# The last 64 tokens of a sequence on all 128 rows of TensorE, in an attention and two MLPs on one Trainium2 core

## The chip, the cores and the metric

The kernel runs on one core of a Trainium2 chip. TensorE multiplies a stationary operand, which a weight load (PEld in the profile) puts into its array of 128 rows and 128 columns, by a moving operand that streams past it (PE in the profile). The contraction runs over the rows. A product over 64 values uses 64 of the rows and is shown as 64*128 in the profile, where the first number is the rows and the second the columns that the stationary operand fills. VectorE (DVE), ScalarE (ACT) and GpSimd (POOL) do the rest of the arithmetic, and SyncE (SP) issues the DMAs, in the order of its queue.

The metric is the device time of one execution in microseconds (us), the median of several runs.

## The reference

An attention in two steps over 8 batches of 8 heads with 576 tokens of 64 values each, in float32, and two MLPs behind it:

```python
def sm_attn(qq, kk, vv):
    s = scale * np.matmul(qq, kk.transpose(0, 1, 3, 2))
    s = s - np.max(s, axis=-1, keepdims=True)
    a = np.exp(s)
    a = a / (np.sum(a, axis=-1, keepdims=True) + 1e-09)
    return np.matmul(a, vv)
p_packed = sm_attn(p, k, v)             # p: 32 rows a head
out = sm_attn(q, p_packed, p_packed)    # 576 rows a head
...
xn = x / rms * rms_g                    # x: 4608 tokens of 512 values
g = xn @ w_gate
x = silu(g) * (xn @ w_val) @ w_out      # 1536 hidden
h = x @ w_in
out = (h * sigmoid(1.702 * h)) @ w_out  # 2048 hidden
```

576 tokens are four chunks of 128 and one of 64. The 64 tokens of that last chunk are what the change is about.

## The kernel before, in words

**The order of the whole.** The attention is cut into 16 chains, one for each batch and each group g of four heads (`chains`, line 146). Chains 0 to 3 (`n < LEAD`) run at the start, spread out by `start` (line 485), which gives each step a time by hand and sorts by it. Chains 4 to 15 run beside the first MLP: `stages` (line 526) lists their steps in order, and the loop at lines 1285 to 1322 hands out one step whenever the first MLP has issued a set amount of TensorE work. So TensorE's queue holds the attention's transposes and products in the middle of the first MLP's products (`prods` line 679, `gateval` line 712, `project` line 748). The second MLP (lines 1068 and 1140) follows without any attention in it. A Tile scheduler with a model of the timeline turns this program into the queues of the engines; some instructions are held in program order, among them all loads of chains 4 and up (line 185).

**One chain.** `load_kp`, `load_v` and `load_q` bring the four heads' k, p, v and q. Each has the last 64 tokens in a load of its own: `kn[:REST, NC - 1]` (lines 197 and 206), `vs[1]` (line 226), `qn[:REST, NC - 1]` (line 240), with NC = 5 and REST = 64. In chains 0 to 3 k comes first as one wide tile, kw, and VectorE puts it in order (line 200). SP issues all loads.

`heads_t` (line 285) transposes k or q, for a pair of heads a and one half e of the chunks: half 0 holds chunks 0 and 1, half 1 holds chunks 2, 3 and 4. Each transpose (line 297) loads the chunk as the stationary operand and streams the identity past it. For chunk 4 the stationary operand is 64 rows high and the identity is cut to 64x64. `scores` (line 308) gives the scores of the packed rows, `s1` their softmax weights e1. `a_t` (line 333) transposes e1 in the same two halves; for chunk 4 the stationary operand has 128 rows and 64 columns, and the 64 rows that come out are copied by two instructions of their own (line 345), apart from those for the other chunks (line 343). `split_v` (line 243) splits v into a high and a low part from chain 4 on, in two pieces: the four full chunks, and chunk 4 on 64 partitions (lines 251 to 255). `pv` (line 347) sums weights by v over the five chunks; from chain 4 on each chunk takes three products (high by high, high by low, low by high), and those of chunk 4 are 64 rows high (line 355). In chains 0 to 3 the operands are plain float32, and the profile shows two instructions for a chunk.

`x` (line 431) makes the rows' sums of squares; its last chunk has 128 rows and 64 columns. `scale` (line 463) transposes the inverse norms ri for each chunk; for the last one (line 474) the stationary operand again has 64 rows.

**Which instructions have 64 rows.** Two transposes of k and two of q in each chain (a = 0 and 1 with e = 1), the products of chunk 4 in `pv`, and one transpose in `scale` for each of the 8 batches.

Of the kernel before, what the change touches and what calls it, by code (L numbers as in the profile page):

```python
# [26 lines left out]
def fl(t):  # L27

    return t.bitcast(F32)
# [3 lines left out]
def tile_pack_attention__then__two_mlps(  # L33
# [14 lines left out]
    nc = tc.nc  # L48
    B, H, S, D = q.shape
# [8 lines left out]
    P = 128  # L58
    HS = S // 2
    TS = 2 * S // 3  # L60
    NC = -(-S // P)
    REST = S - (NC - 1) * P
# [85 lines left out]
    def attention(at, first, lp, psum, getL, getAT):  # L148
# [31 lines left out]
        def load(n, dst, src):  # L180


            i = nc.sync.dma_start(dst, src)
            if n >= LEAD:
                tc.keep_in_program_order(i)

        def load_kp(n):
            at = early(n)
            b, g = chains[n]
            h0, odd = HG * g, b % 2  # L190
            nb = KQ if n < LEAD else 2
            kn = at.tile([P, NC, HG, D], F32, tag="kq", name="kn", bufs=nb)
            rest = k[b, h0 : h0 + HG, S - REST :].rearrange("h p d -> p h d")
            if n < WIDE:
                kw = at.tile([P, HG, NC - 1, D], F32, tag="kq", name="kw", bufs=nb)
                load(n, kw, k[b, h0 : h0 + HG, : S - REST].rearrange("h (p c) d -> p h c d", c=NC - 1))
                load(n, kn[:REST, NC - 1], rest)
                for a in range(2):
                    hs = slice(2 * a, 2 * a + 2)
                    nc.vector.tensor_copy(kn[:, : NC - 1, hs].rearrange("p c h d -> p h c d"), kw[:, hs])  # L200
            else:
                for h in range(HG):
                    load(n, 
                        kn[:, : NC - 1, h, :], k[b, h0 + h, : S - REST].rearrange("(p c) d -> p c d", c=NC - 1)
                    )
                load(n, kn[:REST, NC - 1], rest)
            pb = at.tile([P, HG, D], F32, tag="pb", name="pb", bufs=bufs(n))
            for s in range(2):
                hs = h0 + 2 * (s ^ odd)
                load(n,   # L210
                    pb[64 * s : 64 * s + 64],
                    p[b, hs : hs + 2].rearrange("h n d -> (h n) d").unsqueeze(1).to_broadcast([64, HG, D]),
                )
            st[n].update(kn=kn, pb=pb)

        def load_v(n):
            at = early(n)
            b, g = chains[n]
            tag, nb = ("kq", KQ) if n < LEAD else ("vn", 1)
            vn = at.tile([P, NC, HG, D], F32, tag=tag, name="vn", bufs=nb)  # L220
            vn = vn.rearrange("p c h d -> p (c h d)")
            head = (NC - 1) * HG * D
            vs = vn[:, :head].rearrange("p (h c d) -> p h c d", h=HG, d=D), vn[:REST, head:]
            hs = slice(HG * g, HG * g + HG)
            load(n, vs[0], v[b, hs, : S - REST].rearrange("h (p c) d -> p h c d", c=NC - 1))
            load(n, 
                vs[1].rearrange("p (h d) -> p h d", h=HG), v[b, hs, S - REST :].rearrange("h p d -> p h d")
            )
            st[n]["vn"] = vn

        def load_q(n):
            b, g = chains[n]
            qn = at.tile([P, NC, HG, D], F32, tag="kq", name="qn", bufs=2)
            hs = slice(HG * g, HG * g + HG)
            rest = q[b, hs, S - REST :].rearrange("h p d -> p h d")
            for h in range(HG):
                load(n, 
                    qn[:, : NC - 1, h, :], q[b, HG * g + h, : S - REST].rearrange("(c p) d -> p c d", p=P)
                )
            load(n, qn[:REST, NC - 1], rest)  # L240
            st[n]["qn"] = qn

        def split_v(n):
            at = early(n)
            vn = st[n]["vn"]
            if full(n):
                st[n]["v"] = (vn,)
                return
            vh, vl = (at.tile([P, NC * HG * D], F32R, tag=f"v{x}", name=f"v{x}") for x in "hl")
            head = (NC - 1) * HG * D  # L250
            for part in ((slice(None), slice(head)), (slice(REST), slice(head, NC * HG * D))):
                i = nc.scalar.copy(vh[part], vn[part])
                if n == LEAD:
                    tc.keep_in_program_order(i)
                nc.gpsimd.tensor_sub(vl[part], vn[part], fl(vh[part]))
            st[n]["v"] = vh, vl

        def v_of(t, c):

            head = (NC - 1) * HG * D  # L260
            if c < NC - 1:
                return t[:, :head].rearrange("p (h c d) -> p h c d", h=HG, d=D)[:, :, c, :]
            return t[:REST, head:].rearrange("p (h d) -> p h d", h=HG)

        def p_mask(n):
            at = early(n)
# [18 lines left out]
        def heads_t(n, name, a, e):  # L285

            if (a, e) == (0, 0):
                pool, nb = (early(n), bufs(n)) if name == "k" else (at, 1)
                st[n][name + "T"] = [
                    pool.tile([P, 2, S], kind(n), tag=f"T{x}", name=f"{name}T{x}", bufs=nb) for x in marks(n)  # L290
                ]
            src = st[n][name + "n"]
            ps = psum()
            cols = span(e)
            for c in GROUPS[e]:
                o = c * P - cols.start
                nc.tensor.transpose(  # L297
                    ps[:, o : o + size(c)],
                    src[: size(c), c, 2 * a : 2 * a + 2, :].rearrange("p h d -> p (h d)"),
                    ident[: size(c), : size(c)],  # L300
                )
            split([t[:, a, cols] for t in st[n][name + "T"]], ps[:, : cols.stop - cols.start], nc.vector)

# [29 lines left out]
        def a_t(n, e):  # L333
            at = early(n)
            if e == 0:
                st[n]["aT"] = [at.tile([P, NC, P], kind(n), tag=f"aT{x}", name=f"aT{x}", bufs=1) for x in marks(n)]
            e1 = st[n]["e1"]
            ps = psum()
            ps = ps.rearrange("p (c n) -> p c n", n=P)
            for i, c in enumerate(GROUPS[e]):  # L340
                nc.tensor.transpose(ps[: size(c), i], e1[:, c * P : c * P + size(c)], ident)  # L341
            c0, c1 = GROUPS[e][0], min(GROUPS[e][-1] + 1, NC - 1)
            split([t[:, c0:c1] for t in st[n]["aT"]], ps[:, : c1 - c0], nc.vector)
            if NC - 1 in GROUPS[e]:
                split([t[:REST, NC - 1] for t in st[n]["aT"]], ps[:REST, NC - 1 - c0], nc.vector)

        def pv(n):
            pool = early(n)
            b, g = chains[n]
            o = psum()[:, : HG * D]  # L350
            todo = [(c, x, y) for c in range(NC) for x, y in products(st[n]["aT"], st[n]["v"])]
            for i, (c, x, y) in enumerate(todo):
                nc.tensor.matmul(  # L353
                    o,
                    x[: size(c), c],
                    v_of(y, c),
                    start=i == 0,
                    stop=i == len(todo) - 1,
                )
            pp = kept(n, "pph") if full(n) else pool.tile([P, HG * D], F32, tag="pp", name="pp")  # L360
            nc.vector.scalar_tensor_tensor(pp, o, st[n]["r1"], mask[b % 2], op0=ALU.mult, op1=ALU.mult)
            if full(n):
                st[n].update(pp=pp, pps=(pp,))
            else:
                st[n].update(pp=pp, pps=[kept(n, f"pp{x}") for x in "hl"])
                split(st[n]["pps"], pp, nc.gpsimd)
# [96 lines left out]
        def scale(b, *es):  # L463

            ri = batch[b]["ri"]
            srcs = []
            for e in es:
                ps = psum()  # L470
                cols = span(e)
                for c in GROUPS[e]:
                    o = c * P - cols.start
                    nc.tensor.transpose(
                        ps[:, o : o + size(c)],
                        ri[: size(c), c : c + 1].to_broadcast([size(c), P]),
                        ident[: size(c), : size(c)],
                    )
                srcs.append((cols, ps[:, : cols.stop - cols.start]))
            for g in range(NG):  # L480
                for cols, src in srcs:
                    A = getAT(b // 2)[b % 2][g][:, cols]
                    nc.vector.scalar_tensor_tensor(A, A, math.sqrt(DM), src, op0=ALU.mult, op1=ALU.mult)
# [890 lines left out]
```

## Time and profile before

| | |
|---|---|
| time, median of 3 runs | 1620.88 us (1620.12 to 1622.61) |
| the profiled execution: its time | 1620.02 us |
| the profiled execution: span, first to last instruction | 1618.2 us |
| TensorE busy (PE) / its weight loads (PEld) | 1593.0 us / 1510.4 us |
| VectorE, ScalarE, GpSimd busy | 1094.5, 870.6, 915.7 us |
| granted TensorE clock, mean | 0.998 of 2.4 GHz |
| mean DMA rate | 215 GB/s |

How to read it: busy times of engines overlap, so they don't add up. A busy PE is modelled: an instruction's time reaches from its start to the modelled end of its results, and the next one starts before that. So what an instruction costs TensorE is read from the distance between starts, not from its busy time. PEld's idle time is measured between weight loads, with what ended it in brackets.

### The profile page before, as it was taken

Reading aid. Unit: us, or ns where it says so; the run is one execution under the profiler, and the core shown is the slowest. Engines: PE = TensorE matmul, PEld = TensorE weight load, DVE = VectorE, ACT = ScalarE, POOL = GpSimd, SP = SyncE. Lnnn points to the kernel's source line nnn. Section 1 sums busy time; section 2 is a strip of 40 time slices with the busy share of each in tenths; the row PEclk is TensorE's granted clock in tenths of the full one; section 3 lists DMA queues with packets and bytes.
Section 4 is the critical chain, followed back from the end, with each engine's and each line's share of the span. In section 5 each row is a group of like instructions: output and inputs, shape, how many; then the busy total and the mean of one; then the engine's idle time right before and its main releaser. Section 6 shows DMA issues by size and latency. Waiting matters only on the chain.

```text
span 1618.2 us, 29102 instructions
## 1 busy us (share of the span) xinstructions
PE 1593.0 (98%) x10608; PEld 1510.4 (93%) x10608; DVE 1094.5 (68%) x1899; ACT 870.6 (54%) x1799; POOL 915.7 (57%) x749
## 2 busy tenths in 40 slices
PE   7999999999999999999999999999999999999998
PEld 5699999999999999999999899999999999999998
DVE  5777777767777766676775567754685467468466
ACT  5677777666566655665665353534344434435432
POOL 3547777656655566563655275664466445546442
PEclk9999999999999999999999999999999999999999
DMA  9766666775556665475454887786677667888874
GB/s 263 222 175 185 210 198 215 255 222 184 180 176 210 204 193 180 150 250 204 153 204 149 316 282 241 235 248 187 183 225 248 189 186 240 288 247 252 285 232 143
DMA packets 217725, 348.21 MB, mean 215 GB/s; under 512 B 93936, under 2 KB 123632, under 8 KB 211440
## 3 DMA queue, kind: packets, MB, share of 16 engines
q1 hardware_dynamic: 217584, 346.35, 66.9%
q8 instruction: 85, 1.39, 0.4%
q14 instruction: 56, 0.46, 0.1%
HBM read 279.19 MB, written 67.11 MB: 214 GB/s over the span
## 4 chain that ended last, share of the span: by engine, by line
PE 90%; DMA 2%; DVE 2%; ACT 2%; issue 2%; POOL 1%; SPq 0%; POOLq 0%; DVEq 0%; ACTq 0%
PE ps_dn L1140 21%; PE ps_up L1068 20%; PE ps_o L748 18%; PE ps_g L712 18%; PE ps_w L679 4%; PE ps_at L308 3%; PE ps_at L297 2%; PE ps_at L353 2%; PE ps_at L443 2%; DMA kw<-in_k_dram 1%; DMA vn<-in_v_dram 1%; POOL ol L1114 1%; PE ps_at L341 0%; DMA raw<-in_moe_w_out_dram 0%; DVE Wl L684 0%
## 5 line engine op out<-in xcount | busy, mean ns | idle before, releaser
L1114 POOL TENSOR_TENSOR ol<-g,oh 128x1024 fp32r<-128x1024 f32 (+1 forms) x117 | 258.9, 2223 | 295.7 <-ACT oh L1112 292.9
L1140 PE MATMUL ps_dn<-wo,oh 128*128 128x256 f32 x2016 | 366.2, 283 | 1.8 <-ACT oh L1112 0.9
L1140 PEld LDWEIGHTS ps_dn<-wo,oh 128*128 128x128 f32 x2016 | 318.6, 191 | 8.7 <-ACT oh L1112 1.3
L748 PE MATMUL ps_o<-Hh,wo 128*128 128x384 f32 x1152 | 320.3, 340 | 0.1
L1140 PE MATMUL ps_dn<-wo,ol 128*128 128x256 f32 x1008 | 279.6, 284 | 0.9 <-POOL ol L1114 0.9
L712 PE MATMUL ps_g<-Aqh,Wh 128*128 128x288 f32 x768 | 231.7, 302 | 4.0 <-DVE th L722 2.7
L712 PE MATMUL ps_g<-Aql,Wh 128*128 128x288 f32 x768 | 226.2, 295 | 0.0
L712 PE MATMUL ps_g<-Aqh,Wl 128*128 128x288 f32 x768 | 226.0, 295 | 0.0
L734 POOL TENSOR_TENSOR Hl<-th,Hh 128x576 fp32r<-128x576 f32 x96 | 138.4, 1442 | 138.3 <-ACT Hh L733 138.1
L1068 PE MATMUL ps_up<-x_t,wi 128*128 128x512 f32 (+1 forms) x936 | 213.6, 368 | 0.0
L748 PEld LDWEIGHTS ps_o<-Hh,wo 128*128 128x128 f32 x1152 | 209.9, 188 | 2.1 <-DVE th L725 0.3
L748 PE MATMUL ps_o<-Hl,wo 128*128 128x384 f32 x576 | 194.2, 337 | 0.0
L1140 PEld LDWEIGHTS ps_dn<-wo,ol 128*128 128x128 f32 x1008 | 190.7, 192 | 2.2 <-POOL ol L1114 1.5
L1091 ACT ACTIVATE g<-g 128x512 f32<-128x512 f32 (+1 forms) x120 | 70.7, 589 | 219.9 <-DVE g L1088 120.0
L684 DVE TENSOR_TENSOR Wl<-ps_w,Wh 64x512 fp32r<-64x512 f32 x192 | 131.8, 687 | 82.6 <-ACT Wh L683 79.8
L1068 PEld LDWEIGHTS ps_up<-x_t,wi 128*128 128x128 f32 x936 | 166.1, 188 | 18.7
L763 POOL TENSOR_TENSOR acc<-acc,add 128x384 f32<-128x384 f32 x135 | 139.0, 1041 | 50.1 <-ACT add L761 48.8
L1068 PE MATMUL ps_up<-x_b,wi 128*128 128x512 f32 (+1 forms) x702 | 164.4, 368 | 0.0
L1112 ACT CAST oh<-g 128x1024 fp32r<-128x1024 f32 (+1 forms) x120 | 113.4, 961 | 94.6 <-PE ps_dn L1140 63.4
L683 ACT CAST Wh<-ps_w 64x512 fp32r<-64x512 f32 x192 | 111.7, 582 | 81.7 <-PE ps_w L679 50.3
L712 PEld LDWEIGHTS ps_g<-Aqh,Wh 128*128 128x128 f32 x768 | 144.1, 188 | 8.2 <-DVE th L722 3.2
L1167 DVE TENSOR_TENSOR acc<-acc,ps_dn 128x512 f32<-128x512 f32 (+1 forms) x160 | 99.0, 630 | 71.9 <-PE ps_dn L1140 62.1
(203 smaller groups left out, 3258.3 us busy)
## 6 DMA issues: line engine op xcount, KB each, us to landing
wo<-wo SPq DMA_DIRECT2D x188, 512.0 KB, 4.0
wi<-wi SPq DMA_DIRECT2D x274, 256.0 KB, 3.8
wg<-wg SPq DMA_DIRECT2D x48, 1024.0 KB, 6.4
raw<-in_moe_w_out_dram SPq DMA_DIRECT2D x28, 512.0 KB, 4.4
wi<-stage SPq DMA_DIRECT2D x24, 512.0 KB, 4.1
wo<-stage SPq DMA_DIRECT2D x24, 512.0 KB, 3.7
x<-acc SPq DMA_DIRECT2D x32, 288.0 KB, 3.4
vn<-in_v_dram SPq DMA_DIRECT2D x16, 512.0 KB, 6.8
```

Of the source, the lines that this page charges most:

```text
L683: nc.scalar.copy(Wh[rows, :, g], src)
L684: nc.vector.tensor_sub(Wl[rows, :, g], src, fl(Wh[rows, :, g]))
L712: nc.tensor.matmul(ps, st[:, o, g, c * P : (c + 1) * P], mv[:, g, cols], start=n == 0, stop=n == 3 * NG - 1)
L734: nc.gpsimd.tensor_sub(Hl, th, fl(Hh))
L748: nc.tensor.matmul(ps, st[:, m * P : (m + 1) * P], mv[:, cols], start=n == 0, stop=n == 3 * len(ss) - 1)
L763: nc.gpsimd.tensor_add(a, a, t)
L1068: nc.tensor.matmul(o, w[:, y, k], x[:, z, k], start=i == 0 and not go_on, stop=i == 5, skip_group_check=bool(go_on))
L1091: nc.scalar.activation(gf, o if q == "a12" else gf, AF.Gelu_apprx_sigmoid)
L1112: nc.scalar.copy(oh, src)
L1114: (nc.vector if late else nc.gpsimd).tensor_sub(ol, src, fl(oh))
L1140: nc.tensor.matmul(o[:, r], x[:, a, (r0 + r) * P : (r0 + r + 1) * P], w[:, a, y], start=i == 0 and not go_on, stop=i == 6 * m - 1, skip_gr ...
L1167: nc.vector.tensor_add(z, z, o[:, :m])
```

## The change

Everything on the last chunk is done on 128 rows. The last 64 tokens of k and q are loaded twice, into partitions 0 to 63 and 64 to 127, by two DMAs (`last`), so the transposes of chunk 4 read 128 rows; they write 128 columns, of which the first 64 are used. The last 64 tokens of v go to partitions 64 to 127, and GpSimd sets partitions 0 to 63 of them to zero. `a_t` transposes the last 128 columns of e1 (tokens 448 to 575) as its last chunk, so the weights of tokens 448 to 511 meet the zeros of v in `pv`. With whole partitions, `a_t` copies its second half with one pair of instructions where there were two, and `split_v` splits v with one pair where there were two. `scale` transposes all 128 rows of ri. `x` is as before.

```diff
+        def twice(src):
+            return src.rearrange("h p d -> p h d").unsqueeze(0).to_broadcast([P // REST, REST, HG, D])
+
+        def last(n, dst, src):
+            for i in range(P // REST):
+                load(n, dst[i * REST : (i + 1) * REST], src[i])
...
# load_kp (both ways) and load_q (the same with qn)
-            rest = k[b, h0 : h0 + HG, S - REST :].rearrange("h p d -> p h d")
+            rest = twice(k[b, h0 : h0 + HG, S - REST :])
-                load(n, kn[:REST, NC - 1], rest)
+                last(n, kn[:, NC - 1], rest)
...
# load_v
-            vs = vn[:, :head].rearrange("p (h c d) -> p h c d", h=HG, d=D), vn[:REST, head:]
+            vs = vn[:, :head].rearrange("p (h c d) -> p h c d", h=HG, d=D), vn[P - REST :, head:]
+            nc.gpsimd.memset(vn[: P - REST, head:], 0.0)
...
# split_v
-            for part in ((slice(None), slice(head)), (slice(REST), slice(head, NC * HG * D))):
-                i = nc.scalar.copy(vh[part], vn[part])
-                nc.gpsimd.tensor_sub(vl[part], vn[part], fl(vh[part]))
+            i = nc.scalar.copy(vh, vn)
+            nc.gpsimd.tensor_sub(vl, vn, fl(vh))
...
# heads_t (and scale the same way, with ri)
-                    ps[:, o : o + size(c)],
-                    src[: size(c), c, 2 * a : 2 * a + 2, :].rearrange("p h d -> p (h d)"),
-                    ident[: size(c), : size(c)],
+                    ps[:, o : o + P],
+                    src[:, c, 2 * a : 2 * a + 2, :].rearrange("p h d -> p (h d)"),
+                    ident,
...
# a_t
-                nc.tensor.transpose(ps[: size(c), i], e1[:, c * P : c * P + size(c)], ident)
-            c0, c1 = GROUPS[e][0], min(GROUPS[e][-1] + 1, NC - 1)
+                c1 = c * P + size(c)
+                nc.tensor.transpose(ps[:, i], e1[:, c1 - P : c1], ident)
+            c0, c1 = GROUPS[e][0], GROUPS[e][-1] + 1
             split([t[:, c0:c1] for t in st[n]["aT"]], ps[:, : c1 - c0], nc.vector)
-            if NC - 1 in GROUPS[e]:
-                split([t[:REST, NC - 1] for t in st[n]["aT"]], ps[:REST, NC - 1 - c0], nc.vector)
...
# pv
-                    x[: size(c), c],
+                    x[:, c],
```

## Rows read from the trace of the kernel before

**Rows 1.** Stretches: us, busy us of each engine (instructions), PE clock, DMA share, GB/s

```profile
0.00:40.00 40.00, 30.49 (x146) 21.89 (x147) 21.36 (x60) 22.12 (x62) 12.17 (x26) 1.00 0.98 263
...
76.00:300.00 224.00, 222.95 (x1527) 214.13 (x1526) 171.59 (x370) 166.73 (x387) 162.65 (x161) 1.00 0.63 196
300.00:720.00 420.00, 418.85 (x2884) 406.01 (x2883) 306.02 (x643) 258.33 (x613) 255.59 (x271) 1.00 0.61 200
```

**Rows 2.** Chain that ended last, the start: start us, length us, what

```profile
25.65 6.90 DMA kw<-in_k_dram
...
36.09 0.64 PE ps_at L297 x3
```

**Rows 3.** Timeline of PE around 253 us; a merged row names its first shape

```profile
252.68 0.58 PE L297 MATMUL ps_at<-ident,kn 128*128 128x128 f32 x3
...
253.47 0.33 PE L748 MATMUL ps_o<-Hl,wo 128*128 128x384 f32 x1
```

**Rows 4.** Timeline of PE around 397 us; the last three transposes are one half of a_t

```profile
396.74 0.71 PE L341 MATMUL ps_at<-ident,e 128*128 128x128 f32 x5
397.21 0.42 PE L748 MATMUL ps_o<-Hh,wo 128*128 128x384 f32 x1
397.47 0.33 PE L748 MATMUL ps_o<-Hl,wo 128*128 128x384 f32 x1
```

**Rows 5.** Timeline of PEld: idle time before a load and its releaser in brackets

```profile
252.99 0.13 PEld L297 LDWEIGHTS ps_at<-ident,kn 64*128 64x128 f32 x1 [0.17 <-issue]
...
397.30 0.19 PEld L748 LDWEIGHTS ps_o<-Hl,wo 128*128 128x128 f32 x1
```

**Rows 6.** Instructions by line, 76 to 720 us: count, ns min/median/max, first and last, shapes

```profile
L297 PE MATMUL ps_at<-ident,kn x120: 270/272/328, 81.1 to 648.8; 128*128 128x128 f32 x96, 64*128 64x64 f32 x24
L297 PE MATMUL ps_at<-ident,qn x120: 270/272/276, 88.5 to 675.8; 128*128 128x128 f32 x96, 64*128 64x64 f32 x24
...
L353 PE MATMUL ps_at<-vh,aTh x60: 279/283/390, 98.8 to 681.2; 128*128 128x256 f32 x48, 64*128 64x256 f32 x12
...
L474 PE MATMUL ps_at<-ident,ri x35: 266/272/275, 78.7 to 717.3; 128*128 128x128 f32 x28, 64*128 64x64 f32 x7
...
L341 PE MATMUL ps_at<-ident,e x60: 270/272/276, 93.8 to 666.0; 128*128 128x128 f32 x48, 128*64 128x128 f32 x12
```

**Rows 7.** Timeline of PE around 364 us, the last products of pv

```profile
363.24 0.28 PE L353 MATMUL ps_at<-vl,aTh 128*128 128x256 f32 x1
363.36 0.28 PE L353 MATMUL ps_at<-vh,aTl 128*128 128x256 f32 x1
363.56 0.38 PE L353 MATMUL ps_at<-vh,aTh 64*128 64x256 f32 x1
...
364.46 0.28 PE L679 MATMUL ps_w<-wg,Ll 128*128 128x256 f32 x1
```

**Rows 8.** Timeline of PE: first and last stretch of 64-row products in pv

```profile
100.33 0.39 PE L353 MATMUL ps_at<-vh,aTh 64*128 64x256 f32 x1
...
682.16 0.38 PE L353 MATMUL ps_at<-vh,aTl 64*128 64x256 f32 x1
```

**Rows 9.** Chain that ended last, around 110 us

```profile
102.99 7.73 DMA vn<-in_v_dram
...
117.30 1.05 PE ps_g L712 x6
```

**Rows 10.** Lines 297 and 353, 36 to 62 us: idle before its loads; instructions

```profile
  issue: 1.4, 6
...
L353 PE MATMUL ps_at<-vn,aTh x20: 376/379/480, 43.3 to 55.2; 128*128 128x256 f32 x16, 64*128 64x256 f32 x4
```

**Rows 11.** Timeline of SP's queue at the start

```profile
1.22 0.70 SPq L183 DMA_DIRECT2D kn<-in_k_dram  x1
```

**Rows 12.** Waits of SP's queue, 76 to 720 us: us in total, times, longest

```profile
SPq L654 <- PE ps_w L679: 63.6, 11, 22.6
```

**Rows 13.** Groups of instructions on POOL: busy us, mean ns, idle us before

```profile
masks.py:197 POOL MEMSET ident<- 128x128 f32 x1 | 0.2, 205 | 0.3 <-POOLq L1358 0.3
```

More of the change, by code (lines that the diff above doesn't have):

```diff
@@ L205, in load_kp @@
                     )
-                load(n, kn[:REST, NC - 1], rest)
+                last(n, kn[:, NC - 1], rest)
             pb = at.tile([P, HG, D], F32, tag="pb", name="pb", bufs=bufs(n))
@@ L234, in load_q @@
             hs = slice(HG * g, HG * g + HG)
-            rest = q[b, hs, S - REST :].rearrange("h p d -> p h d")
+            rest = twice(q[b, hs, S - REST :])
             for h in range(HG):
@@ L239, in load_q @@
                 )
-            load(n, qn[:REST, NC - 1], rest)
+            last(n, qn[:, NC - 1], rest)
             st[n]["qn"] = qn
@@ L249, in split_v @@
             vh, vl = (at.tile([P, NC * HG * D], F32R, tag=f"v{x}", name=f"v{x}") for x in "hl")
-            head = (NC - 1) * HG * D
-            for part in ((slice(None), slice(head)), (slice(REST), slice(head, NC * HG * D))):
-                i = nc.scalar.copy(vh[part], vn[part])
-                if n == LEAD:
-                    tc.keep_in_program_order(i)
-                nc.gpsimd.tensor_sub(vl[part], vn[part], fl(vh[part]))
+            i = nc.scalar.copy(vh, vn)
+            if n == LEAD:
+                tc.keep_in_program_order(i)
+            nc.gpsimd.tensor_sub(vl, vn, fl(vh))
             st[n]["v"] = vh, vl
@@ L262, in v_of @@
                 return t[:, :head].rearrange("p (h c d) -> p h c d", h=HG, d=D)[:, :, c, :]
-            return t[:REST, head:].rearrange("p (h d) -> p h d", h=HG)
+            return t[:, head:].rearrange("p (h d) -> p h d", h=HG)
         def p_mask(n):
@@ L474, in scale @@
                     nc.tensor.transpose(
-                        ps[:, o : o + size(c)],
-                        ri[: size(c), c : c + 1].to_broadcast([size(c), P]),
-                        ident[: size(c), : size(c)],
+                        ps[:, o : o + P],
+                        ri[:, c : c + 1].to_broadcast([P, P]),
+                        ident,
                     )
```

## The prediction

> **What bounds the kernel now.** I read the busy times by stretch first, because the change touches only the attention, which ends near 720 us. From 76 to 720 us TensorE is busy 641.8 of 644 us, at the full clock, while ScalarE, VectorE and GpSimd stay between 61 and 77% of each stretch [rows 1]. So there TensorE's queue is the bound, and any time that one of its instructions takes from the next is paid in full. The first 40 us are another case: TensorE is busy 30.5 us of them, the DMA engines 98%, at 263 GB/s [rows 1], and the chain that ended last goes through the k loads of chains 0 to 3 until TensorE takes over at 36.1 us [rows 2]. A busy TensorE hides pauses, so next I read the distances between starts.
>
> **What a 64-row instruction costs.** At 252.68 us three transposes of k start, the third with 64 rows, and a product of project follows; the second product starts at 253.47, 0.79 us after the first transpose [rows 3]. The same sequence without 64 rows stands in a_t: five transposes in a row, busy 0.71 us together, so with 0.27 us for the last one they start 0.11 us apart. The third of the five starts at 396.96, the second product behind them at 397.47, 0.51 us later [rows 4]. The 64-row transpose costs 0.28 us. The load side shows where it goes: the weight load of 64 rows begins only after 0.17 us of idle, whose cause is shown as issue, that is nothing the profile knows [rows 5]. TensorE seems to run empty before it and again after it. The last transposes of a_t have 128 rows and 64 columns [rows 6] and show no such pause [rows 4], so it is the rows that matter. In pv the products start 0.12 us apart; with the three of 64 rows between, the six steps from 363.36 to 364.46 take 1.10 us and not 0.72 [rows 7]: 0.38 us for a stretch of them.
>
> **The change, part by part.**
> The transposes in heads_t: 24 of k and 24 of q have 64 rows after 76 us [rows 6]. All become like their neighbours. The doubled columns (64 to 128) are inside the 0.11 us of a_t's transposes, which stream 128 already [rows 6]. 48 x 0.28 = 13.4 us less.
> The transposes in scale: 7 after 76 us [rows 6], taken like those of heads_t: 2.0 us less.
> The products of pv: 12 chains with three each [rows 6]. Where products of the MLP stand between them, one chain pauses twice; I count 18 stretches, the first at 100.33 and the last, one product alone, at 682.16 [rows 8]. 18 x 0.38 = 6.8 us less.
> Together 22.2 us off TensorE's queue.
> Its cover: the other engines' waits fill only 2.2 of the 644 us [rows 1], so nearly all is real, except where another chain sets the pace. One such place is a v load that lands late: the chain goes through it from 102.99 until TensorE is back at 117.30 [rows 9]. What is saved between 76 and 117 us (five transposes and one stretch of pv, 5 x 0.28 + 0.38) may only lengthen that wait: 1.8 us given back.
> The start, saving: TensorE is on the chain from 36 us on [rows 2], and up to 62 us its loads in heads_t pause six times, while pv has two chains' 64-row products, two instructions each [rows 10]. At the same prices 6 x 0.28 + 2 x 0.38 = 2.4 us less.
> The start, loss: before the last k load on the chain is issued at 25.65 [rows 2], five more small loads go to SP (k of chains 0, 1 and 2, q of 0 and 1). Each is 64 rows of four heads, 65.5 KB. By the DMA rate of that stretch, 263 GB/s [rows 1], that is 0.25 us each, 1.3 us in all. By SP's own issue time, 0.70 us for such a load [rows 11], it is 3.5 us, if the queue's head and not the engines sets the landing; at the lower end it is nothing, if the loads fit into gaps. I take 1.3, since the engines are 98% busy and a load therefore waits for bytes more than for its issue.
> The Trainium skill ("DMA: Bandwidth & Descriptors", Issuing engines are not separate DMA queues) says that a sequencer's time to start a DMA is usually small beside the transfer. By that, bytes alone count and the sum stays as it is; by the row the issue of 0.70 us is longer than the 0.25 us of the bytes, so the higher end stays in my range.
> Loads after 76 us: 24 more on SP, at 0.70 us 17 us of issue in 644. SP waits there 63.6 us for TensorE to free gate weights alone [rows 12], so the time is covered; behind each load stand that chain's p or the next weights. Without that cover a weight load would be late by 0.7 us.
> GpSimd's 16 memsets of 64x256: none of that size is in the trace. The 128x128 one took 0.21 us [rows 13]; at twice the columns 0.4. GpSimd has the slack for it (73% busy at most) and a v load takes 7.73 us to land in the one place where it is late [rows 9], so I take nothing on the path; at most 12 x 0.4 = 5 us, if each held up SP and TensorE in turn.
> The merged copies in a_t and split_v save an instruction each on ScalarE, VectorE and GpSimd, which are not the bound: nothing, and a gain at most where the 2.2 us of waits are.
>
> **The sum.** -22.2 + 1.8 - 2.4 + 1.3 = -21.5 us. The profiled execution took 1620.02 us, which makes 1598.5; the median of the runs shown is 0.86 above it, so I forecast 1599.4 us.
>
> **Against it, by a rule.** Loads of 128 rows begin while a product on all 128 rows still runs: at 397.30 one begins behind the product that runs from 397.21 for 0.42 us [rows 4, 5].
> The Trainium skill ("TensorE: Matmul & The Clock Gate", Part 3, The mechanism) states that a weight load overlaps a running matmul only when their row groups differ. By that a 64-row instruction could have neighbours in the other rows and a full one could not. The trace disagrees, in the pause of 0.17 us and in the overlap just named.
>
> **Rivals.**
> 1. Half of it comes back. ScalarE is at 74%, VectorE at 77% and GpSimd at 73% from 76 to 300 us [rows 1], and bursts of them could take over once TensorE is quicker. For it: the wait at 103 to 117 us is one. Against: it is the one large one. 1620.9 - 11 = 1610 us.
> 2. The pause is not of the rows but of something that stays, say of the end of a group: no gain, 1621 us. Against: a_t ends a group as well and has none [rows 4].
> 3. Slower: the memset holds up SP. GpSimd's queue is in order; if the v load is made to wait for the memset in the same tile, SP stands still while GpSimd finishes what is before it, and the weight loads behind come late. It decides once TensorE waits 22.2 / 12 = 1.9 us in each chain. With 2.7 us each it is 1621 + 12 x 0.8 = 1630 us. Against: the slack of SP's queue [rows 12].
> 4. A 128-row load in the place of a 64-row one overlaps nothing, and TensorE waits for all of it: 55 x 0.13 + 36 x 0.19 = 14.0 us, with 0.13 us for the load of a transpose and 0.19 for that of a product [rows 5]: 1635 us. Against: the loads of 128 rows that do overlap [rows 4, 5]. This is what the Trainium skill's sentence above would come to.
>
> **How the numbers follow.** 0.2%, 3.2 us, is about what a measurement of this kernel can tell from no change. The forecast has 0.76, rival 1 0.12, rival 2 0.05, rival 3 0.06, rival 4 0.01. Faster is the forecast and rival 1, 0.88; the same is rival 2, 0.05; slower are rivals 3 and 4, 0.07. The low end of the range is the sum with nothing lost at the start and nothing given back (1596.3) and another tenth of the 22.2 us, for prices read from rows rounded to 0.01 us: 1594. The high end is rival 1, 1610, which also holds the start's higher price (1601.6) and the memsets' 5 us. That leaves out 0.12.
>
> **What would show it.** Right: in heads_t, scale and pv all shapes read 128*128, the pauses shown as issue are gone from lines 297, 353 and 474, a transpose follows the last within 0.11 us, a stretch of pv steps by 0.12 us, and the end of the attention moves up by some 20 us while the second MLP keeps its length. The k load of chain 3 lands one to three us later. Wrong: pauses that stay at the new 128-row instructions; TensorE waiting in many places for ScalarE or VectorE (rival 1); weight loads that land after their first use, behind a v load that waits for GpSimd (rival 3).

## The result, and the profile of the changed kernel

The changed kernel takes 1602.42 us, the median of 4 runs (1601.84 to 1603.62), against 1620.50 us for the kernel before (4 runs, 1620.08 to 1622.61). The ratio is 0.9889, with a 95% interval from 0.9876 to 0.9901: 18.1 us faster, where 21.5 were worked out. The profiled execution is 17.62 us shorter (1602.40 against 1620.02).

The first view is the timeline of TensorE in the changed kernel (start us, length us, line, operands, rows*columns, idle time before it).

```profile
19.06 3.93 PE L360 MATMUL ps_at<-vn,aTh 128*128 128x256 f32 x10 [2.18 <-ACT aTh L162]
...
173.70 0.49 PE L305 MATMUL ps_at<-ident,qn 128*128 128x128 f32 x3
173.95 0.42 PE L755 MATMUL ps_o<-Hl,wo 128*128 128x384 f32 x1
174.21 0.33 PE L755 MATMUL ps_o<-Hh,wo 128*128 128x384 f32 x1
...
360.03 0.28 PE L360 MATMUL ps_at<-vl,aTh 128*128 128x256 f32 x1
360.14 0.28 PE L360 MATMUL ps_at<-vh,aTl 128*128 128x256 f32 x1
360.26 0.39 PE L686 MATMUL ps_w<-wg,Lh 128*128 128x256 f32 x2
```

Line 305 was line 297 and line 360 was line 353. Three transposes, then the second product behind them: 0.51 us from 173.70 to 174.21, where it was 0.79 [rows 3]. The last products of pv step by 0.11 to 0.12 us, chunk 4 among them, where the same stretch lost 0.38 us [rows 7]. The row at 19.06 belongs to the start, below.

The weight loads show the same. The groups of PEld by line, 76 to 720 us, first of the kernel before (busy us, mean ns of one, idle us before them and what ended it):

```profile
L297 PEld LDWEIGHTS ps_at<-ident,qn 128*128 128x128 f32 (+1 forms) x120 | 15.6, 139 | 4.3 <-issue 4.0
L341 PEld LDWEIGHTS ps_at<-ident,e 128*128 128x128 f32 (+1 forms) x60 | 7.1, 134 | 0.3
L474 PEld LDWEIGHTS ps_at<-ident,ri 128*128 128x128 f32 (+1 forms) x35 | 4.4, 134 | 1.3 <-issue 1.2
```

and of the changed kernel:

```profile
L305 PEld LDWEIGHTS ps_at<-ident,qn 128*128 128x128 f32 x120 | 15.2, 140 | 0.7 <-ACT e L335 0.2
L305 PEld LDWEIGHTS ps_at<-ident,kn 128*128 128x128 f32 x120 | 15.1, 140 | 0.6 <-DVE kTl L164 0.2
L360 PEld LDWEIGHTS ps_at<-vh,aTh 128*128 128x128 f32 x60 | 11.3, 188 | 0.0
L481 PEld LDWEIGHTS ps_at<-ident,ri 128*128 128x128 f32 x35 | 4.2, 136 | 0.5 <-POOL ri L467 0.5
```

One shape is left in each group, and no idle time is put down to issue. So the change does what it says everywhere. What was lost is in the stretches of the changed kernel (columns as in [rows 1]):

```profile
0.00:66.00 66.00, 52.45 (x263) 41.86 (x264) 38.15 (x100) 37.36 (x106) 26.97 (x53) 0.97 0.94 266
...
20.00:22.00 2.00, 2.00 (x7) 1.55 (x6) 1.30 (x2) 1.31 (x3) 1.23 (x1) 0.50 1.13 311
...
76.00:300.00 224.00, 220.97 (x1566) 217.06 (x1565) 173.06 (x370) 168.06 (x382) 166.27 (x167) 1.00 0.66 204
300.00:703.00 403.00, 400.95 (x2847) 398.18 (x2846) 300.59 (x631) 253.39 (x593) 252.53 (x264) 1.00 0.64 206
```

From 76 to 703 us TensorE is idle 5.1 us where it was 2.2 of a longer stretch [rows 1]. The waits of TensorE on others, 76 to 745 us, say for whom (us in total, times, longest), in the kernel before:

```profile
PE ps_at L281 <- POOL pbm L269: 0.8, 1, 0.8
PE ps_g L712 <- DVE Wl L684: 0.8, 1, 0.8
PE ps_g L712 <- DVE th L725: 0.3, 1, 0.3
PE ps_g L712 <- ACT Wh L683: 0.2, 1, 0.2
```

and in the changed kernel:

```profile
PE ps_g L719 <- DVE th L732: 1.6, 2, 1.3
PE ps_g L719 <- DVE Wl L691: 1.1, 1, 1.1
PE ps_at L289 <- POOL pbm L277: 0.8, 1, 0.8
PE ps_w L686 <- DVE Wl L691: 0.6, 1, 0.6
PE ps_g L719 <- DVE acc L765: 0.2, 1, 0.2
PE ps_g L719 <- DVE w L131: 0.2, 1, 0.2
PE ps_at L481 <- POOL ri L467: 0.2, 1, 0.2
```

That is 2.1 us before and 4.7 after; 3.7 of the 4.7 are for VectorE.

**Where along the run.** I lined up the n-th product of a kind in both traces. At 66.6 us of the kernel before the changed one is 0.6 us late. It is 5.3 us early at 229 us, still only 4.3 at 406, 13.8 at 662 and 16.7 at 742, the end of the attention. By the end it is 17.6 ahead. Between 229 and 406 us nothing is gained.

To split this I summed every distance between starts in excess of the usual one for that sequence of shapes (all excesses over 0.12 us): a measure of all of TensorE's waits, a little wider than the profile's. It gives 3.4 us before and 7.8 after, from 66.6 to 742 us. The changed kernel gained 16.66 + 0.59 = 17.25 us there and waited 4.4 more, so the pauses that went were worth 21.6 us.

| term, us | worked out | measured in the profiled executions |
|---|---|---|
| pauses gone after 66 us | -22.2 | -21.6 |
| TensorE's waits | +1.8 | +4.4 |
| start, to 66 us | -1.1 | +0.6 |
| behind the attention | 0 | -1.0 |
| sum | -21.5 | -17.6 |

### The profile page after: what moved, and what is told of

Same layout as the page of the kernel before. It is cut to its first block, busy times and chain, and to the rows that moved or that the text cites. A ratio compares the mean times of both kernels' runs of the same rounds, so it can differ in the third digit from the quotient of the medians.

```text
span 1600.6 us, 29125 instructions
## 1 busy us (share of the span) xinstructions
PE 1569.7 (98%) x10608; PEld 1506.5 (94%) x10608; DVE 1089.1 (68%) x1887; ACT 867.2 (54%) x1771; POOL 917.9 (57%) x753
## 4 chain that ended last, share of the span: by engine, by line
PE 90%; DVE 3%; ACT 3%; issue 2%; DMA 1%; POOL 1%; SPq 1%; POOLq 0%; ACTq 0%; DVEq 0%
PE ps_dn L1147 22%; PE ps_up L1075 22%; PE ps_g L719 17%; PE ps_o L755 17%; PE ps_w L686 4%; PE ps_at L316 3%; PE ps_at L360 2%; PE ps_at L305 2%; PE ps_at L450 2%; DMA vn<-in_v_dram 1%; SPq L183 1%; ACT ps_at L459 1%; DVE Wl L691 1%; PE ps_at L350 0%; ACT Wh L690 0%
## 5 line engine op out<-in xcount | busy, mean ns | idle before, releaser
L770 POOL TENSOR_TENSOR acc<-acc,add 128x384 f32<-128x384 f32 x135 | 138.5, 1036 | 42.5 <-ACT add L768 41.6
```

What stands on the lines that cost most here:

```text
L770: nc.gpsimd.tensor_add(a, a, t)
```

## The experiments

All times are medians. Each kernel was timed beside the kernel before on the same chip; it took 1620.05 us for the first four (15 runs), 1620.61 for the next four (9), 1620.46 for the three after them (15) and 1619.35 for the last one (7). Start is the shift at 66.6 us, waits and pauses gone are split as above, v is ScalarE's time in waits for the DMA of v from 76 to 745 us.

| kernel | us (lowest to highest) | ratio and 95% interval | start | waits | pauses gone | v |
|---|---|---|---|---|---|---|
| before | as above | 1 | 0 | 3.4 | 0 | 4.9 |
| changed | 1602.42 (1601.84 to 1603.62) | 0.9889, 0.9876 to 0.9901 | +0.6 | 7.8 | 21.6 | 9.1 |
| heads alone | 1605.62 (1604.25 to 1607.54) | 0.9911, 0.9897 to 0.9924 | +1.6 | 3.5 | 17.0 | 6.9 |
| pv alone | 1616.93 (1615.80 to 1618.63) | 0.9983, 0.9974 to 0.9992 | +0.4 | 7.1 | 6.6 | 10.0 |
| more stretches | 1628.30 (1627.35 to 1631.21) | 1.0052, 1.0039 to 1.0064 | +3.2 | 2.9 | -8.7 | 1.9 |
| one load | 1601.37 (1600.08 to 1603.01) | 0.9881, 0.9866 to 0.9896 | 0.0 | 8.3 | 21.6 | 8.7 |
| zeros | 1609.80 (1606.86 to 1610.74) | 0.9929, 0.9917 to 0.9942 | +0.8 | 12.3 | 21.2 | 13.3 |
| split in two | 1604.12 (1603.04 to 1604.81) | 0.9898, 0.9883 to 0.9913 | +2.1 | 7.3 | 22.0 | 10.7 |
| GpSimd in two | 1602.74 (1601.18 to 1603.52) | 0.9887, 0.9873 to 0.9900 | +1.9 | 5.8 | 21.9 | 5.2 |
| GpSimd in five | 1603.54 (1602.71 to 1604.94) | 0.9894, 0.9880 to 0.9907 | +0.4 | 7.4 | 21.4 | 12.3 |
| early v | 1601.71 (1599.48 to 1603.86) | 0.9889, 0.9874 to 0.9904 | +0.8 | 5.3 | 21.4 | 3.2 |
| before, early v | 1620.17 (1617.88 to 1621.58) | 0.9995, 0.9985 to 1.0005 | -0.4 | 3.8 | 0.3 | 3.3 |
| three together | 1597.82 (1596.83 to 1598.44) | 0.9862, 0.9849 to 0.9876 | 0.0 | 3.4 | 22.3 | 3.3 |
| three, late v | 1601.05 (1600.09 to 1603.27) | 0.9887, 0.9867 to 0.9906 | -0.8 | 7.0 | 21.6 | 8.4 |

### The prices: one part at a time, and one part made worse

**Heads alone** keeps the doubled loads and the transposes of heads_t and scale of the changed kernel and puts v, a_t, split_v and pv back.

```diff
-            nc.gpsimd.memset(vn[: P - REST, head:], 0.0)
...
-                    x[:, c],
+                    x[: size(c), c],
```

> Only the transposes of heads_t and scale on 128 rows (with the second loads of k and q); v, a_t, split_v and pv as before. Theory (each return from 64 to 128 rows costs TensorE a pause, 0.28 us for a transpose; the start loses some 3 us because the extra loads stand ahead of the first gate weights in SP's queue): 55 x 0.28 = 15.4 us off the queue, 1.7 saved and 2.9 lost at the start, 1 to 3 us come back as waits: 11 to 14 us less than before, 1607 to 1610 us. Rival (the pause belongs to the products of pv or to the shorter copies): under 5 us less, over 1615 us.

**Pv alone** is the kernel before with only those parts changed (zeros and last tokens of v in rows 64 to 127, a_t, split_v, pv).

```diff
+            nc.gpsimd.memset(vn[: P - REST, head:], 0.0)
...
-                    x[: size(c), c],
+                    x[:, c],
```

> Only v, split_v, a_t and pv on 128 rows; the transposes and loads of k and q as before. Theory: 18 stretches x 0.38 = 6.8 us and 0.8 at the start, no extra loads and so no loss there, about 1 us back as waits: 6 to 7.5 us less, 1613 to 1615 us; the first products of pv start near 17.5 us as before. Rival (the saved copies on ScalarE and VectorE, not the rows, are what helps): the gain would not show as shorter steps within pv.

**More stretches** is the kernel before with the three 64-row products of pv each among 128-row ones, so that there are 36 stretches in place of 18.

```diff
+            if not full(n):
+                todo = [*todo[:3], todo[12], *todo[3:6], todo[13], *todo[6:9], todo[14], *todo[9:12]]
```

> The kernel before with the three 64-row products of a chain's pv set apart from each other, between those of the full chunks: 36 stretches where there were 18, with the same instructions. Theory (the cost is per change of height): 18 x 0.38 = 6.8 us more than before, 1626 to 1628 us. Rival (the cost is per 64-row instruction, however they stand): no change, 1620 to 1622 us.

Heads alone took 1605.62 us, 1.4 below the band that was expected, and pv alone 1616.93, 1.9 above its own. With the waits taken out, the pauses that went are 17.0 and 6.6 us, where the prices said 15.4 and 6.8. Part of the surplus of heads alone is in the order of its work: its timeline has 15 stretches of 64-row products in pv where the kernel before has 18, and 3 x 0.38 is 1.1 us. More stretches took 1628.30, just over its band; its profiled execution is the slowest of its five, 1631.21 us. That trace loses 6.57 us from 92 to 742 us, where 18 x 0.38 = 6.8 was expected. The rest of its loss lies earlier: 3.2 us by 66.6, with two stretches of half the granted clock (0.50 from 17.7 to 21.1 and from 38.2 to 41.6 us), and 1.6 from 66 to 92, in a stretch with half of the clock granted for part of the time:

```profile
75.00:85.00 10.00, 8.91 (x43) 6.77 (x44) 5.82 (x13) 6.42 (x18) 5.08 (x7) 0.83 0.43 158
```

So a change of height in the array costs what the rows said, in both directions. The two parts differ in their waits: the part with the transposes has 3.5 us of them, as before (3.4), though it made TensorE 17 us quicker; pv alone has 7.1, though it made it only 6.6 quicker. So in these two kernels the new waits come with what the change does to v and not with TensorE's speed as such. Each of them has its own order of the work, too, so this pair alone does not show it.

### The start: loads and zeros

**One load** is the changed kernel with k's and q's last chunk by a single load of the last 128 tokens, which also lie in chunk 3.

```diff
-            for i in range(P // REST):
-                load(n, dst[i * REST : (i + 1) * REST], src[i])
+            load(n, dst, src)
...
-            rest = twice(k[b, h0 : h0 + HG, S - REST :])
+            rest = k[b, h0 : h0 + HG, S - P :].rearrange("h p d -> p h d")
...
-            for c in GROUPS[e]:
-                o = c * P - cols.start
+            for c in sorted(GROUPS[e], key=lambda c: (c + 1) % NC):
+                o = c * P + size(c) - P - cols.start
```

> The changed kernel, but the last chunk of k and q comes as one load of the last 128 tokens instead of two loads of 64; the transpose of that chunk is written first and the one of chunk 3 over its first 64 columns. The bytes are those of the changed kernel, the number of loads that of the kernel before. Theory (the start loses by the number of loads ahead of the first gate weights): that weight load is issued near 11.9 us and not 13.5, the first pv starts near 17.5 and not 19.1 us and the granted clock does not fall there; 2 to 3 us less than the changed kernel, 1599 to 1600.5 us. Rival (the bytes are what costs): the same as the changed kernel, 1602 to 1603 us.

**Zeros** loads the last 64 tokens once and has GpSimd write zeros beside them.

```diff
-            for i in range(P // REST):
-                load(n, dst[i * REST : (i + 1) * REST], src[i])
+            nc.gpsimd.memset(dst[REST:], 0.0)
+            load(n, dst[:REST], src)
...
# rest of k and of q: as in the kernel before, without twice()
```

> The changed kernel with k's and q's last 64 tokens loaded once, as before, and GpSimd's zeros in the other 64 rows. If SP's issue of the second loads at the start delays the first raw gate weights (issued at 13.51 us in place of 11.89) and with them ScalarE, pv of chain 0 and TensorE's clock: raw weights issued at 11.9, pv of chain 0 at 17.5, 1599.5 to 1601.5. If that delay is paid back by the stretches after it: 1602 to 1603; if the zeros on GpSimd delay the loads instead: over 1603.

One load gave 1601.37 us, above its band; by the ratios it can't be told from the changed kernel. The three signs that were expected of it did not come: the first raw gate weights are issued at 12.75 us (11.9 expected), pv of chain 0 starts at 18.30 (17.5 expected), and the granted clock falls all the same (0.50 from 18.9 to 22.2 us). With as many loads as before and the pauses gone, its start is as long as the start before (0.0), not 2.4 us shorter. The table has more of it: the three kernels with one load start 0.8 us early to 0.0 (mean -0.3), the six with two loads 0.4 to 2.1 us late (mean +1.2). So the second loads cost some 1.5 us there, and a saving of 2.4 us does not show. One load alone can't part the two, since it still moves the doubled bytes; but zeros, which has neither second loads nor their bytes, starts 0.8 us late too. TensorE is busy 2.8 us less from 0 to 66 us than in this row of the kernel before, and the stretch is no shorter; it is idle 2.8 us more:

```profile
0.00:66.00 66.00, 55.26 (x265) 39.96 (x265) 39.95 (x101) 37.93 (x111) 25.90 (x48) 1.00 0.95 267
```

How the loads reach TensorE is on the chain that ended last in the changed kernel, 10 to 20 us (start us, length us, what):

```profile
12.86 0.60 SPq L1269
...
13.51 4.17 DMA raw<-in_moe_w_gate_dram
...
17.77 0.62 ACT between L129
18.39 0.35 ACT kTh L162
18.74 0.28 ACT aTh L162
...
19.06 0.94 PE ps_at L360 x3
```

SP issues the first raw gate weights at 13.51 us; in the kernel before it does so at 11.89, with three small loads fewer ahead of them. ScalarE, in order, waits for those weights, and the copy of aTh that pv of chain 0 needs stands behind that wait. TensorE is idle 2.18 us (0.62 before). After that idle time the granted clock fell to its lower level, 1.2 GHz (0.50 from 20 to 22 us above), and the ten products took 3.93 us, against 2.62 before. The fall is not bound to the second loads: it came in pv alone, whose gate weights are issued at 11.89 us as before (1.56 us idle, the ten products 3.99 us, 0.50 from 17.3 to 20.6 us), and not in zeros, where TensorE was idle 2.38 us at that place (2.43 us for the products, 1.00 from 10 to 26 us). Most of the delay is paid back by 66.6 us.

Chain 3's wide k load is issued at 25.65 us in the kernel before [rows 2], at 28.11 in the changed one (27.27 to 28.66 in the six kernels with two loads, mean 28.0) and at 26.29 to 27.47 with one load (mean 26.9). The kernels that load those 64 rows once issue it at 25.44 to 26.44. Against 25.65, five loads of 64 rows more delay it by 2.35 us on average, 0.47 each; 1.2 us of that stays where the same bytes come by five larger loads, and 1.1 goes with the second issue.

Zeros took 1609.80 us, 7.4 us over the changed kernel, by its size the last of its cases. The waits of GpSimd's queue, 76 to 745 us, point to a reason:

```profile
POOL vl L263 <- ACT vh L260: 30.0, 8, 8.8
...
POOL qn L193 <- PE ps_at L305: 7.0, 3, 3.8
...
POOL kn L193 <- PE ps_at L305: 2.6, 1, 2.6
```

The zeros can only be written once the transposes that read the old tile are done, and GpSimd stands 9.6 us in its queue for that. That this makes ScalarE's and VectorE's results late is argued from the order of GpSimd's queue, not shown step by step; ScalarE's waits for v (13.3) and TensorE's (12.3) are the largest of all kernels.

### The merged copies of v

In the changed kernel GpSimd subtracts 128x1280 in one instruction. Its timeline around 318 us:

```profile
318.39 2.95 POOL L263 TENSOR_TENSOR vl<-vn,vh 128x1280 fp32r<-128x1280 f32 x1 [1.84 <-ACT vh L260]
```

and VectorE's:

```profile
318.62 3.00 DVE L904 TENSOR_TENSOR sums<-w 128x256 f32<-128x256 f32 x1
321.55 0.74 DVE L408 TENSOR_REDUCE mx<-t 128x18 f32<-128x576 f32 x1
```

A VectorE subtraction of two SBUF tiles, begun 0.23 us into GpSimd's, ends 0.28 us behind it. My theory was that this hold-up makes the waits. Three kernels cut the instructions up again.

**Split in two**: ScalarE's copy and GpSimd's subtraction in two pieces.

```diff
-            i = nc.scalar.copy(vh, vn)
-            if n == LEAD:
-                tc.keep_in_program_order(i)
-            nc.gpsimd.tensor_sub(vl, vn, fl(vh))
+            head = (NC - 1) * HG * D
+            for part in (slice(head), slice(head, NC * HG * D)):
+                i = nc.scalar.copy(vh[:, part], vn[:, part])
+                if n == LEAD:
+                    tc.keep_in_program_order(i)
+                nc.gpsimd.tensor_sub(vl[:, part], vn[:, part], fl(vh[:, part]))
```

> The changed kernel with split_v in two pieces again (1024 columns, then 256), on all 128 rows, so that ScalarE's copy and GpSimd's subtraction are as long as before. If the merged pieces bring back what is lost in the middle of the attention (a gain of 5.3 us at 229 us that is 4.3 at 406, where the two parts of the change should have made it some 11): 1598.5 to 1600, and TensorE's waits on other engines from 76 to 720 us fall from 4.7 us to about 2. If those waits are only a chance of the order, or come from the second split of a_t or the zeros: 1602 to 1603.

**GpSimd in two**: the subtraction alone.

```diff
-            nc.gpsimd.tensor_sub(vl, vn, fl(vh))
+            head = (NC - 1) * HG * D
+            for part in (slice(head), slice(head, NC * HG * D)):
+                nc.gpsimd.tensor_sub(vl[:, part], vn[:, part], fl(vh[:, part]))
```

> The changed kernel with only GpSimd's subtraction of split_v in two pieces, ScalarE's copy merged as in the changed kernel. If the loss in the middle is VectorE standing still under GpSimd's one subtraction of 2.95 us: 1599 to 1600.5, and no VectorE instruction of 128x256 takes over 2.5 us. If it is ScalarE's merged copy (1.27 us, waiting for the whole of v with other work queued behind it): 1601.5 to 1602.5, with the first kernel of this call at 1599 to 1600.

**GpSimd in five**: ScalarE's copy in two pieces, the subtraction in five.

```diff
# ScalarE's copy: as in split in two
...
-            nc.gpsimd.tensor_sub(vl, vn, fl(vh))
+            for c in range(NC):
+                part = slice(c * HG * D, (c + 1) * HG * D)
+                nc.gpsimd.tensor_sub(vl[:, part], vn[:, part], fl(vh[:, part]))
```

> The changed kernel with ScalarE's copy in two pieces and GpSimd's subtraction in five of 256 columns (0.75 us each by rows of that shape). If VectorE stands still for as long as one GpSimd instruction lasts: its longest excess falls to about 0.7 us, and 1597.5 to 1599.5, below the kernel with two pieces. If the length of one GpSimd instruction does not matter: within 0.5 us of the kernel with two pieces, or above it by the 0.8 us more that five pieces occupy GpSimd.

In the last of them GpSimd's five pieces begin at 318.69, 3.71 us in all, and the timeline of VectorE has the same subtraction right behind that:

```profile
319.21 0.51 DVE L908 TENSOR_TENSOR sums<-w 128x256 f32<-128x256 f32 x1
319.64 0.74 DVE L412 TENSOR_REDUCE mx<-t 128x18 f32<-128x576 f32 x1
```

0.51 us in place of 3.00: VectorE is held for one GpSimd instruction, not for the work as a whole. But the times are 1604.12, 1602.74 and 1603.54 us, none below the changed kernel (GpSimd in two equals it by the ratios, 0.9887 and 0.9889); the first two lie above both of their cases, the third in its second. Of the waits of the changed kernel from 299 to 367 us only one or none is left, but those at 245 to 251 us stayed and new ones came, at 283, 531 or 547 us. The hold-up is real, and in the changed kernel the chain that ended last goes through it: through the subtraction at 318 us to TensorE's waits at 328 and 335 us, and through another at 362.70 (2.32 us, behind GpSimd's at 361.80) to the one at 366, 1.7 us of the 4.7 in all. But as these waits went, others came, and the time did not fall: as an account of the time lost my theory fell.

### When v arrives

Over the kernels up to here ScalarE's time in waits for v goes roughly along with TensorE's waits; the clearest exception is heads alone. In `stages` the next chain's v is loaded behind pv and split a few steps later, and ScalarE's copy of it waits with other work behind it in its queue. **Early v** loads it three steps sooner. In three together, below, SP so issues chain 5's v at 95.96 us, where the changed kernel issues it at 103.70.

```diff
-                do((heads_t, n, "q", 1, 0))
+                do((heads_t, n, "q", 1, 0), *([(load_v, m)] if m else []))
...
-                    do((load_v, m), (load_q, m), (p_t, m))
+                    do((load_q, m), (p_t, m))
```

> The changed kernel with the loads of the next chain's v issued three steps earlier (beside the first transposes of q's second half, in place of behind pv). ScalarE's waits for v from 76 to 745 us went along with TensorE's waits on other engines over the kernels so far (1.9 us with 1.8, 4.9 with 2.1, 9.1 with 4.7, 13.3 with 9.3). If the one causes the other: ScalarE's waits for v under 3 us in place of 9.1, TensorE's waits at 2 to 3 us in place of 4.7, 1599 to 1600.5. If TensorE's waits come from where the scheduler's order happens to put the work: 1601.5 to 1604, with ScalarE's waits for v gone all the same.

**Before, early v** makes the same edit in the kernel before.

> The kernel before with the same earlier loads of v. By the first theory it has little to gain, since its TensorE waits only 2.1 us on others, 0.8 of it on GpSimd's mask: 1619 to 1620.5. By the second: 1619 to 1623, by chance of the order.

**Three together** is the changed kernel with early v, one load and GpSimd in two, by the diffs above.

> The changed kernel with the earlier loads of v, with k's and q's last chunk by one load of the last 128 tokens (some 1 us less by its own run), and GpSimd's subtraction of split_v in two pieces (TensorE's waits 3.6 us in place of 4.7 in its own run). If these parts add up: 1597.5 to 1599.5, below both kernels. If the order decides: 1600.5 to 1603.

**Three, late v** takes the early v out of that again.

> The fastest kernel so far without its earlier loads of v: one load for k's and q's last chunk and GpSimd's subtraction in two pieces alone. If the late v is what costs, and the earlier loads gave the fastest kernel its time: ScalarE's waits for v back at 5 to 9 us in place of 3.3, 1600 to 1602. If it was the subtraction in pieces, or the order in which the scheduler puts the work: 1597 to 1599.

Early v cut ScalarE's waits for v from 9.1 to 3.2 us and TensorE's from 7.8 to 5.3, but its median of 1601.71 us misses its band, with runs from 1599.48 to 1603.86: no difference that this shows. The kernel before gained nothing from it, as expected, but its trace holds two things that cancel: 14 stretches of 64-row products in place of 18 (4 x 0.38 = 1.5 us), and 1.6 us lost from 66.6 to 76 us, where the granted clock was 0.51 from 72.4 to 75.9. Three together took 1597.82, in its band and below both kernels (the interval of its ratio ends at 0.9876, where that of the changed kernel begins), and its waits are those of the kernel before (3.4). The waits of TensorE on others there, 76 to 745 us, are three:

```profile
PE ps_at L306 <- DVE qTl L164: 1.1, 1, 1.1
PE ps_g L720 <- DVE th L730: 1.1, 1, 1.1
PE ps_at L290 <- POOL pbm L278: 0.8, 1, 0.8
```

With v late again and nothing else changed they are six:

```profile
PE ps_g L720 <- DVE Wl L692: 1.6, 1, 1.6
PE ps_g L720 <- DVE th L733: 1.2, 3, 0.5
PE ps_g L720 <- DVE th L730: 1.1, 1, 1.1
PE ps_at L290 <- POOL pbm L278: 0.8, 1, 0.8
PE ps_w L687 <- DVE Wl L692: 0.6, 1, 0.6
PE ps_at L482 <- POOL ri L468: 0.2, 1, 0.2
```

and the time is 1601.05 us, 3.2 more by medians (4.3 with each taken against its own runs of the kernel before, 22.6 us of gain for 18.3; the intervals of the ratios still overlap). ScalarE's waits for v are back at 8.4. That is what the theory of the late v said for this pair, at 1600 to 1602. The chain that ended last says the same. In the changed kernel it goes through two loads of v after 76 us and from each of them, by way of ScalarE's copy, to a wait of TensorE (1.1 us at 117.10, 0.6 at 249.81); the last row is the held subtraction:

```profile
104.17 6.96 DMA vn<-in_v_dram
...
117.10 2.62 PE ps_g L719 x18
...
237.79 5.66 DMA vn<-in_v_dram
...
249.81 0.95 PE ps_w L686 x6
...
318.70 2.93 DVE sums L904
```

With v early (early v and three together) the chain goes through no load of v there, in three, late v through three (102.74, 184.24 and 237.61 us). In pv alone it goes through two, in heads alone through none, which fits its few waits.

So the late v is shown as a cause of the waits, beside the held subtractions. What it costs in time rests on one pair of kernels. It stays open how much of that is the scheduler's order, which every edit shifts a little: early v alone did not bring its time down.

## Why the prediction was right, and where it was off

**What bounds the kernel** was right. TensorE's queue was full from 76 to 720 us, and most of what was taken off it came off the time: the end of the attention moved up by 16.7 us, where some 20 were foreseen. 1602.4 us is in the range, 3.0 above the forecast.

**The prices of a 64-row stretch** were right, the main terms with them. All nine kernels that hold the whole change lost 21.2 to 22.3 us of pauses by the split above, against 22.2. More stretches cost 6.57 us, where 6.8 was worked out. That the rows matter and not the columns is borne out by the groups of PEld: the transposes of 128 rows have no such idle time left, the last transposes of a_t (128*64, in L341 above) had none before.

The pause on both sides of a change of height fits a sentence that I had not weighed. The Trainium skill ("TensorEngine Tiling (Array Packing)", Tiling Modes, Key Properties) says that changing the tiling mode drains TensorE. The traces agree that there is a pause, of 0.28 us for a transpose and 0.38 us for a stretch of pv; that it is this drain they do not show, and the Trainium skill gives no time there. The rule that I had weighed against the change, rival 4 (the Trainium skill, "TensorE: Matmul & The Clock Gate", Part 3, The mechanism), is out: the 128-row loads overlap [rows 4, 5], and the kernel with them is 18.1 us faster.

**The cover, "nearly all is real, except where another chain sets the pace", failed in its size.** I named one place, the v load at 103 to 117 us, and gave 1.8 us back. In kind it was right: TensorE is back at 117.10 us where it was 117.30 [rows 9], with 1.05 us of lead just before it, so 0.85 us was given back there. But other places came; together the waits grew by 4.4 us. One more is the mechanism that I named (v late, ScalarE behind it), at 249.81 us; the waits from 328 to 366 us come by another, VectorE held by GpSimd, which I had not counted. This is rival 1 in small: 2.6 us more than foreseen came back, not 11.

**The start's saving of 2.4 us failed.** TensorE did lose 2.8 us of busy time before 66 us, but the stretch stayed as long; with one load it is -0.3 us on average. I had taken the pauses there as if TensorE's queue were full, though [rows 1] showed it busy 30.5 of the first 40 us; a pause in a queue that waits for data is worth nothing.

**The start's loss of 1.3 us** was about right in size (some 1.5 us for the second loads, by the means above), but only half of its mechanism was. The bytes, 0.25 us a load, answer to the 1.2 us for five loads that one load keeps. SP's second issue comes on top with as much again, where I had taken the one or the other; with 0.47 us a load the upper end of 0.70 [rows 11] was not reached. By the sentence of the Trainium skill that I had weighed ("DMA: Bandwidth & Descriptors", Issuing engines are not separate DMA queues) the issue would count for little; here it is half of the delay. The forecast that this load comes one to three us later was right. I had looked only at it and not at the raw gate weights in the same queue, for which ScalarE waits.

**The memsets** cost nothing on the path by themselves: 64x256 takes 0.305 us (0.4 estimated), and the v load on the chain is issued at 103.70 where it was 102.99, so rival 3 did not come. Zeros in k and q show the danger was not idle: there GpSimd waits in its queue and 7.4 us are lost.

**The merged copies, "nothing",** held by time: cutting them up again gained nothing. In the mechanism it was short: the longer GpSimd instruction holds VectorE, and TensorE waited 1.7 us behind that.

**The second MLP keeps its length**: within 1 us, to the good. That 1.0 us was not foreseen, and it makes the sum look better than its terms: they miss by 0.6, 2.6 and 1.7 us the other way.

## What to carry to other kernels

An operand that fills half of the array's rows among full ones cost TensorE a pause on both sides of it here: compare the distance between starts in a sequence with it and in the same sequence without it, and multiply by the stretches, not by the instructions. The gain counts only where TensorE's queue is full, so cost the stretches that wait for data at nothing, and list each place where a load arrives just in time, for these are where a quicker TensorE gives time back. Fill the missing rows by loading real neighbours in one transfer rather than by zeros from an engine that would have to wait for the buffer.

## What the runs showed that I had not expected

A VectorE subtraction with two SBUF inputs stands still while a GpSimd subtraction runs that began before it: 3.00 us in place of 0.51, to the end of that one instruction. The Trainium skill ("SBUF — State Buffer", Who interferes with whom) states that a VectorE instruction with two SBUF inputs contends with a GpSimd instruction that reads SBUF, and that the order of issue decides which of the two is blocked. The rows at 318 us agree. That the block lasts for a whole instruction the Trainium skill says there only of other VectorE modes; the rows show it for this pair.

In the changed kernel the granted clock fell to its lower level at the start, after 2.18 us of idle TensorE, and the scores behind pv came 2.86 us later (23.21 in place of 20.35): 1.54 us by pv's later start and 1.31 us by its longer run at that clock. What decides whether the clock falls there the runs leave open: it fell in pv alone after 1.56 us of idle time and not in zeros after 2.38.
